# Weights converted in place, tokens mixed by rows, one rotated tile fewer and a new order of the start

## The chip, the cores and the metric

One Trainium2 chip; the program runs on one core. The metric is the device time of that core in microseconds, the median of several runs. TensorE (PE) does the matrix products, VectorE (DVE) and ScalarE (ACT) the elementwise work, GpSimd (POOL) a few small operations and the indirect loads, and SyncE (SP) issues the DMAs.

## The reference

Three layers follow each other on tensors of 4 batches, 768 tokens and 384 columns (8 heads of 48):

```python
# 1. attention with a complex decay, per batch and head
mag = np.sqrt(a_re * a_re + a_im * a_im)
scale = np.minimum(mag, 0.999) / (mag + 1e-06)
for t in range(S):                       # a = (a_re, a_im) * scale
    S_re, S_im = ar * S_re - ai * S_im + k_t v_t^T, ar * S_im + ai * S_re
    y[t] = q_t @ S_re
# 2. token mixing of rank 32, then an MLP 384 -> 1536 -> 384
u = x + (x.transpose(0, 2, 1) @ U @ V).transpose(0, 2, 1)
x = u + np.maximum(u @ w_ch1, 0.0) @ w_ch2
# 3. real part of a 2-D Fourier transform, normalisation, a second MLP
u = x + np.real(np.fft.fft(np.fft.fft(x, axis=1), axis=2))
un = (u - mean) / np.sqrt(var + 1e-06)
out = u + np.maximum(un @ w2_ch1, 0.0) @ w2_ch2
```

All inputs are float64 in memory (two 32-bit words a value) where they are weights, U and V, and float32 for the attention.

## The kernel before

**Pieces of work.** A batch has six chunks c of 128 tokens, and two groups g of three chunks (384 tokens). The attention works on pairs of chunks, numbered m: ACT and DVE make decays, phases, gains and from them a rotated tile QK (128 x 6 x 258; partition = position in a head's 16 columns and head, so 16 x 8). Six DMAs (`move`, L316) bring a QK to a tile QT (96 partitions, 8 heads x 258), each of them one of six blocks (z, i) to 16 neighbouring partitions. From QT come the scores (`sc`, L322), masked on DVE (`pm`), the outputs `y` (L337) and the states. The keys are turned back on PE (`kp`, L330), copied by head on ACT into a key tile (`kc`, L334; L371) and multiplied with the values (`g`). The rotated tiles have three buffers; the key tiles share a ring of three (`st`) with the loaded weights.

**Token mixing.** Six products on PE give z = U^T x of a batch (L384; U stands four times side by side, in parts), ACT copies it to `zst`, DVE subtracts for the low part. For a group and each of three column blocks k, PE transposes three chunks of x (`tokens`, L402), adds V^T z by one product (`mixed`, L414), and ACT and DVE split the result into two float16 tiles u (L1050, L1052): the mixed tokens, turned, are the moving operand of the first product. The residual x does not hold the mixing yet; so after the last second product three products `extra1` (L447) add it to the accumulator, for which ACT scales `zst` (`zsc`).

**MLP.** For each group and each of twelve blocks f (FB) of hidden columns: nine products in float16 parts (`first_product`, L192), ReLU on ACT (`hh`), its low part on DVE (`hl`), then six products with hh and three with hl into three accumulators (`second_product`, L208; L1083, L224). That is 18 matmuls of 384 columns for (group, f), 8 groups and 12 blocks, in both MLPs.

**Weights.** A float64 weight is made a float32 with integer steps (`word_steps`, L131): the sign and exponent word goes through Abs on ACT, the low word is shifted on DVE, and two DVE steps join them into a tile of its own (`slot`, ring `x1`); then ACT and DVE split it into two float16 parts (L163, L164). All this goes by tiles of 128 x 384, two for each (mi, f), 48 in all.

**Order.** The first six groups (batches 0 to 2 of the first MLP) with the attention of all batches are written in an order that is made when the program is built: `planned_start` (L616) describes each operation as a stream entry `op(engine, took, label, *after)`, and `planned` (L521) picks, engine by engine, the entry with the earliest known start plus a bias of its stream (`PLACES`, L486). Each engine and SP then run that order as it is; rings of buffers (`sizes`, L1184) count as waits. Where PE would idle over a unit, `warm_up` (L606) puts filler products in (L609 before the first MLP product, L612 after it). From group (3, 0) on, `moe_units` (L216) runs the rest: a side list (`put`, L1551) puts steps of the Fourier transform, of the last mixing (`make_ut(3, 1)`) and of the normalised inputs (`make_un`) at numbered half steps. `make_un` splits a normalised chunk into float16 parts and turns it with a DMA transpose (L1461).

Of the kernel before, what the change touches and what calls it, by code (L numbers as in the profile page):

```python
# [34 lines left out]
W1_MOST = 1.5  # L35
FOLD, WAVE = 2.0**6, 2.0**-3
# [12 lines left out]
def mixer_kernel(ctx, tc, a_in, qk_in, v_in, u_in, v4_in, w_in, cc_in, ss_in, cb_in, sb_in, id_in, mask_in, rows_in, out):  # L49
# [25 lines left out]

    def pair(name):
        if parts16[0]:
            return moe.tile([128, 2, 384], F16, tag="u", name=name, bufs=5)
        return pfl[0].tile([128, 2, 384], F32R, tag="u32", name=name, bufs=3)
# [45 lines left out]
    def fetch(src, name):  # L125
        n = src.shape[-1]
        st = moe.tile([128, 400, 2], I32, tag="st", name=f"st{name}", bufs=3)[:, :n]
        nc.sync.dma_start(st.rearrange("p n w -> p (n w)"), src.bitcast(I32))
        return st

    def word_steps(st, x):  # L131

        n = x.shape[-1]
# [13 lines left out]
    def words(mi, f, z):  # L147
        return w_in[mi, f][:, z * 384 : (z + 1) * 384], f"w{mi}_{f}_{z}"

    def load_steps(mi, f, z, st):  # L150

        if z == 0 and not parts16[0]:
            wt[mi, f] = wpl.tile([128, 2, 768], F32R, tag="w", name=f"w{mi}_{f}")
        elif z == 0:
# [3 lines left out]
        zs = slice(z * 384, (z + 1) * 384)  # L158
        hi, lo = wt[mi, f][:, 0, zs], wt[mi, f][:, 1, zs]
        x = slot(f"wx{words(mi, f, z)[1]}")  # L160
        if parts16[0]:
            return word_steps(st, x) + [
                ("A", lambda: A.activation(hi, x, AF.Copy, scale=WP[z])),  # L163
                ("V", lambda: V.scalar_tensor_tensor(out=lo, in0=x, scalar=WP[z], in1=hi, op0=ALU.mult, op1=ALU.subtract)),  # L164
            ]
        return word_steps(st, x) + [
            ("A", lambda: A.copy(hi, x)),
            ("G", lambda: G.tensor_tensor(lo, x, f32(hi), ALU.subtract)),
        ]

    def load_w(mi, f, z, st=None):
        for _, fn in load_steps(mi, f, z, fetch(*words(mi, f, z)) if st is None else st):
            fn()
# [8 lines left out]
    def weights(mi):  # L182
        todo = [(f, z) for f in range(FB) for z in range(2)]
        st = None
        for at, (f, z) in enumerate(todo):
            now = fetch(*words(mi, f, z)) if st is None else st
            st = fetch(*words(mi, *todo[at + 1])) if at + 1 < len(todo) else None
            load_w(mi, f, z, now)
            yield

# [25 lines left out]
    def moe_units(todo):  # L216
# [5 lines left out]
        def low(mi, b, g, f, hl, t):  # L222
            last_step = f == FB - 1
            T.matmul(acc[t], hl[:, TSS[t]], wt[mi, f][:, 0, 384:], start=False, stop=last_step and mi == 1)  # L224
            if last_step:
                if mi == 0:
# [75 lines left out]
    def qk_tile(kind, b, c):  # L302
        where = dict(pl=early[0], bufs=1) if c % 3 == 2 else dict(bufs=2)
# [30 lines left out]
    def by_head(ks, ps, z):  # L334
        A.copy(ks[:, :768].rearrange("t (h z x) -> t h z x", h=8, z=2)[:, :, z, :], ps.rearrange("t (x h) -> t h x", h=8))
# [1445 lines left out]
```

## Time and profile before

| | |
|---|---|
| median of 3 runs | 852.25 us (852.24 to 853.67) |
| profiled execution | 851.42 us, of it the span 849.6 us |
| PE busy | 789.3 us (93%), 6875 matmuls |
| DVE busy | 627.7 us (74%), 1304 instructions |
| ACT busy | 451.5 us (53%), 845 instructions |
| POOL busy | 36.7 us (4%) |
| DMA | 87.78 MB, mean 103 GB/s |
| granted TensorE clock | 0.996 of full speed |

The span runs from the first to the last instruction of the profile; the 1.8 us between it and the execution's time lie outside the program's instructions. Busy times are unions of an engine's instructions. A matmul's duration is the time until its result is there, and the next one starts long before that; on a full PE the distance of two starts is what one costs. Releasers (after an arrow) name what ended an engine's idle time.

### The profile page before, as it was taken

How to read it: one execution, taken by the hardware profiler on the slowest of the kernel's cores; microseconds unless marked ns; L12 is line 12 of the kernel's file. 1: busy time of each engine (PE TensorE's matmuls, PEld its weight loads, DVE VectorE, ACT ScalarE, POOL GpSimd, SP SyncE). 2: the span in 40 equal slices, each digit the busy share in tenths (PEclk: the TensorE clock that was granted, in tenths of full speed). 3: DMA queues.
4: the chain of work that ended last, by engine and by line, in shares of the span. 5: the costliest groups of instructions: out<-in, count | busy, mean ns of one | idle time of the engine just before them, and what ended most of it. 6: DMA issues, size and time to landing. Idle time of an engine off the chain costs nothing.

```text
span 849.6 us, 17219 instructions
## 1 busy us (share of the span) xinstructions
PE 789.3 (93%) x6875; PEld 533.1 (63%) x6875; DVE 627.7 (74%) x1304; ACT 451.5 (53%) x845; POOL 36.7 (4%) x79
## 2 busy tenths in 40 slices
PE   0298999999999999999999999999999999999996
PEld 0187755567766677666766666566666666666664
DVE  6989689998788986998965956666475748555653
ACT  7976597798868778848743252242215214321210
POOL 1001000000000010000002200001000100000000
PEclk9999999999999999999999999999999999999999
DMA  9539933487493494268675201211311142010100
GB/s 347 81 73 127 299 104 106 127 164 188 85 188 113 124 210 125 85 158 133 140 140 176 96 21 55 66 29 57 75 47 29 56 103 26 31 29 29 29 29 33
DMA packets 66553, 87.78 MB, mean 103 GB/s; under 512 B 24800, under 2 KB 55776, under 8 KB 66464
## 3 DMA queue, kind: packets, MB, share of 16 engines
q1 hardware_dynamic: 65184, 82.66, 41.0%
q0 software_dynamic: 1280, 3.93, 1.5%
q8 instruction: 56, 0.92, 0.5%
q14 instruction: 33, 0.27, 0.1%
HBM read 53.39 MB, written 9.44 MB: 74 GB/s over the span
## 4 chain that ended last, share of the span: by engine, by line
PE 77%; ACT 10%; DVE 6%; DMA 4%; issue 1%; SPq 1%; DVEq 0%; ACTq 0%
PE acc L210 10%; PE hp L105 10%; PE hp L107 10%; PE acc L211 10%; PE hp L106 10%; PE acc L224 7%; PE sc L325 4%; PE acc L1083 3%; PE y L343 3%; DMA QT<-QK 2%; ACT ain L101 2%; ACT L97 2%; PE g L343 2%; PE kp L332 1%; PE z L385 1%
## 5 line engine op out<-in xcount | busy, mean ns | idle before, releaser
L201 ACT ACTIVATE hh<-hp 128x384 f16<-128x384 f32 x192 | 93.3, 488 | 281.2 <-PE hp L107 270.1
L204 DVE SCALAR_TENSOR_TENSOR hl<-hp,hh 128x384 f16<-128x384 f32 x192 | 105.7, 555 | 126.4 <-ACT hh L201 125.7
L210 PE MATMUL acc<-w,hh 128*128 128x384 f16 x576 | 187.8, 327 | 3.5 <-ACT hh L201 3.4
L211 PE MATMUL acc<-w,hh 128*128 128x384 f16 x576 | 187.4, 326 | 0.0
L105 PE MATMUL hp<-u,w 128*128 128x384 f16 x288 | 94.3, 328 | 0.1
L106 PE MATMUL hp<-u,w 128*128 128x384 f16 x288 | 94.2, 327 | 0.0
L107 PE MATMUL hp<-u,w 128*128 128x384 f16 x288 | 94.2, 327 | 0.0
L105 PE MATMUL hp<-nt,w 128*128 128x384 f16 x288 | 94.1, 327 | 0.0
L107 PE MATMUL hp<-nt,w 128*128 128x384 f16 x288 | 94.0, 327 | 0.0
L106 PE MATMUL hp<-nt,w 128*128 128x384 f16 x288 | 94.0, 326 | 0.0
L210 PEld LDWEIGHTS <-hh 128*128 128x128 f16 x576 | 56.2, 98 | 41.5 <-ACT hh L201 6.1
L105 PEld LDWEIGHTS <-w 128*128 128x128 f16 x576 | 56.4, 98 | 37.8 <-issue 0.5
L107 PEld LDWEIGHTS <-w 128*128 128x128 f16 x576 | 56.3, 98 | 37.4 <-issue 0.2
L106 PEld LDWEIGHTS <-w 128*128 128x128 f16 x576 | 56.4, 98 | 36.8 <-issue 0.7
L211 PEld LDWEIGHTS <-hh 128*128 128x128 f16 x576 | 56.3, 98 | 34.1 <-issue 0.4
L224 PE MATMUL acc<-w,hl 128*128 128x384 f16 x360 | 77.6, 327 | 0.0
L325 PE MATMUL sc<-QT 96*128 96x128 f32 x384 | 50.1, 285 | 10.4 <-DMA QT<-QK 9.6
L325 PEld LDWEIGHTS sc<-QT 96*128 96x128 f32 x384 | 47.1, 198 | 12.8 <-issue 11.5
L332 PE MATMUL kp<-ident,QK 128*128 128x128 f32 x120 | 20.0, 294 | 33.4 <-DVE QK L309 31.1
L1083 PE MATMUL acc<-w,hl 128*128 128x384 f16 x216 | 49.2, 331 | 1.4 <-DVE hl L204 1.4
L224 PEld LDWEIGHTS <-hl 128*128 128x128 f16 x360 | 35.2, 98 | 23.7
L97 ACT ACT_TABLE_LOAD x33 | 42.3, 1283 | 1.3 <-PEq L1767 0.7
(262 smaller groups left out, 1395.3 us busy)
## 6 DMA issues: line engine op xcount, KB each, us to landing
QT<-QK SPq DMA_DIRECT2D x144, 129.0 KB, 6.8
stw<-in_w_dram SPq DMA_DIRECT2D x48, 384.0 KB, 5.2
ain<-in_a_dram SPq DMA_DIRECT2D x12, 768.0 KB, 6.9
qkin<-in_qk_dram SPq DMA_DIRECT2D x12, 768.0 KB, 6.3
x1d<-x SPq DMA_DIRECT2D x24, 192.0 KB, 4.1
vin<-in_v_dram SPq DMA_DIRECT2D x18, 192.0 KB, 3.9
lo<-x1d SPq DMA_DIRECT2D x12, 192.0 KB, 3.6
out_dram<-lo SPq DMA_DIRECT2D x12, 192.0 KB, 2.0
```

The lines of the kernel that those rows point to most:

```text
L97: ordered(lambda: A.preload_act_table_set(name))
L105: T.matmul(o, ah, bh, start=start, stop=False, skip_group_check=skip)
L106: T.matmul(o, ah, bl, start=False, stop=False, skip_group_check=skip)
L107: T.matmul(o, al, bh, start=False, stop=stop, skip_group_check=skip)
L201: A.activation(hh, hp, AF.Relu)
L204: V.scalar_tensor_tensor(out=hl, in0=hp, scalar=0.0, in1=whole_of(hh), op0=ALU.max, op1=ALU.subtract)
L210: T.matmul(acc[t], hh[:, TSS[t]], w[:, 0, 384:], start=f == 0, stop=False)
L211: T.matmul(acc[t], hh[:, TSS[t]], w[:, 1, 384:], start=False, stop=False)
L224: T.matmul(acc[t], hl[:, TSS[t]], wt[mi, f][:, 0, 384:], start=False, stop=last_step and mi == 1)
L325: T.matmul(ps[:, h, :], q[:, 128:256], q[:, :128], start=True, stop=True)
L343: T.matmul(out[p, hsl], l(h)[:, p], r[:, hsl], start=h == 0 and o + done == 0, stop=h == 7 and o + rest == len(ops) - 1, skip_group_check= ...
L1083: T.matmul(accs[t], hls[n][:, TSS[t]], wt[0, every[n][2]][:, 0, 384:], start=False, stop=False)
```

## The change

- Weights: a pair of tiles (768 columns) is loaded into one tile `dw` of a ring of two, by two DMAs, and made float32 in place: the shift, the sign and the last step on DVE write the low words, Abs on ACT the high words, each once over 768 columns. The split into float16 parts stays by 384. V is converted the same way in one piece, U in the buffer of `zst`. The slots of ring `x1` are not used for it any more.
- Rotated tiles: two buffers in place of three, so a chunk waits for the moves and the key turns of the chunk but one before it (instead of but two). QT keeps three.
- A move writes to every sixth partition of QT, starting at z * 3 + i, in place of 16 neighbouring ones; the columns of the key tile are laid out to match. The key tile has a buffer of its own, one, 768 columns wide, without the zeroed rest; so a chunk's key turns come after the state product of the chunk before.
- Mixing: U stands three times instead of four, z has 96 rows. Groups (0, 0), (0, 1) and (1, 0) are mixed as before. For (1, 1), (2, 0), (2, 1), (3, 0) and (3, 1) a product per chunk of tokens gives V^T z by rows, DVE adds it to x, ACT and DVE split the sum, and a DMA transpose turns it. For (1, 0) the product and the addition are made too, after the turned tiles have been read. `extra1` stays for batch 0 alone, as does the scaling of `zst`, which has one buffer now in place of two: its copy for batch 1 waits for the last `extra1` of batch 0, later ones for the last products by rows.
- `make_un(0, 0)`, the first normalised group, is turned by nine transposes on PE instead of three DMA transposes, at other half steps; `make_ut(3, 1)` is at half steps 11, 13 and 15.
- All biases of `PLACES` are others (two lines are shown), and the planner's costs for moves (1.0 to 0.62), for a DMA's start (2.4 to 2.15) and for early filler; so the order of the first six groups is another on every engine.

```diff
+    def turned_tile(name):
+        return moe.tile([128, 2, 3, 384], F16, tag="u", name=name, bufs=2)
...
+    def double_words(name):
+        return (attp[0] if parts16[0] else pfl[0]).tile([128, 768, 2], I32, tag="dw", name=f"st{name}", bufs=2 if parts16[0] else 1)
...
         low, high = st[:, :, 0], st[:, :, 1]
-        xi = x.bitcast(I32)
+        size = high.bitcast(F32)
         return [
-            ("A", lambda: kept(A.activation, x, high.bitcast(F32), AF.Abs, scale=2.0**-112)),
             ("V", lambda: kept(V.tensor_scalar, low, low, 29, None, ALU.logical_shift_right)),
-            ("V", lambda: V.scalar_tensor_tensor(out=xi, in0=xi, scalar=3, in1=low, op0=ALU.logical_shift_left, op1=ALU.bitwise_or)),
-            ("V", lambda: V.scalar_tensor_tensor(out=xi, in0=high, scalar=-(2**31), in1=xi, op0=ALU.bitwise_and, op1=ALU.bitwise_or)),
+            ("V", lambda: V.scalar_tensor_tensor(out=low, in0=high, scalar=-(2**31), in1=low, op0=ALU.bitwise_and, op1=ALU.bitwise_or)),
+            ("A", lambda: kept(A.activation, size, size, AF.Abs, scale=2.0**-112)),
+            ("V", lambda: V.scalar_tensor_tensor(out=low, in0=high, scalar=3, in1=low, op0=ALU.logical_shift_left, op1=ALU.bitwise_or)),
         ]
...
     def qk_tile(kind, b, c):
-        where = dict(pl=early[0], bufs=1) if c % 3 == 2 else dict(bufs=2)
+        where = dict(pl=early[0], bufs=1) if c % 3 == 2 and kind == "QT" else dict(bufs=2)
...
     def move(QT, QK, z, i):
-        p0 = z * 48 + i * 16
-        nc.sync.dma_start(QT[p0 : p0 + 16], QK[:, z, i, :])
+        nc.sync.dma_start(QT[z * 3 + i : 96 : 6], QK[:, z, i, :])
...
     def key_tile(n):
-        ks = moe.tile([128, 800], F32, tag="st", name=f"k{n}", bufs=3)
-        G.memset(ks[:, 768:], 0.0)
+        ks = attp[0].tile([128, 768], F32, tag="ks", name=f"k{n}", bufs=1)
...
+        for n in range(3):
             if parts16[0]:
-                A.activation(u[:, 0], xp, AF.Copy, scale=UP)
-                V.scalar_tensor_tensor(out=u[:, 1], in0=xp, scalar=UP, in1=u[:, 0], op0=ALU.mult, op1=ALU.subtract)
+                up = bank(f"up{b}_{g}_{n}")[:, :DM]
+                low_rank_back(up, b, 3 * g + n)
+                V.tensor_tensor(xt[b, 3 * g + n], up, xt[b, 3 * g + n], ALU.add)
+                n16 = split_tile(f"un{b}_{g}_{n}")
+                high_part(n16, xt[b, 3 * g + n])
+                low_part(n16, xt[b, 3 * g + n])
+                turn_over(nt, n16, n)
...
+    def low_rank_back(acc, b, c, start=True):
+        T.matmul(acc, vst[:96, c * 128 : (c + 1) * 128], zst[b][:96], start=start, stop=True)
...
+    def high_part(n16, x, scale=UP):
+        A.activation(n16[:, 0], x, AF.Copy, scale=scale)
+
+    def low_part(n16, x, scale=UP):
+        V.scalar_tensor_tensor(out=n16[:, 1], in0=x, scalar=scale, in1=n16[:, 0], op0=ALU.mult, op1=ALU.subtract)
+
+    def turn_over(nt, n16, t):
+        to = nt.rearrange("d z k t -> d (z k) t")[:, :, TSS[t]]
+        nc.sync.dma_start_transpose(out=to, in_=n16.rearrange("t z d -> t (z d)"))
...
-        "moves": (154, 157, 56),
+        "moves": (97, 209, 151),
...
+        "mixed_tokens": (-155, -109, -84),
...
-                free["Q"] = max(free["Q"], t + 2.4) + took
+                free["Q"] = max(free["Q"], t + 2.15) + took
...
-            for _ in range(int(us / 0.11)):
+            for _ in range(int(us / (0.11 if "sc2.0" in known else 0.15))):
...
-                if c > 2:
-                    before += [f"qt{c - 3}"] + ([f"kp{c - 3}.1"] if turned_too(c - 3) else [])
+                if c > 1:
+                    before += [f"qt{c - 2}"] + ([f"kp{c - 2}.1"] if turned_too(c - 2) else [])
...
-                    yield op("S", 1.0, f"qt{c}" if at_end else f"qt{c}.{z}{i}", *before)
+                    yield op("S", 0.62, f"qt{c}" if at_end else f"qt{c}.{z}{i}", *before)
...
-                yield op("P", 0.35, f"kp{c}.{z}", f"QKk{c}", "ident", *room_for(c), holds=[(ring, f"kc{c}.{z}")])
+                yield op("P", 0.35, f"kp{c}.{z}", f"QKk{c}", "ident", *room_for(c), *[f"g{x}" for x in (c - 1, c - 2)[: 1 + (c % NC == 0)] if x >= 0 and turned_too(x)], holds=[(ring, f"kc{c}.{z}")])
...
-            yield op("A", 0.42, f"zh{b}", f"z{b * NC + NC - 1}", *([f"ex{b - 2}.1.2"] if b > 1 else []))
-            z = zst[b] = xpl[0].tile([128, DM], F32R, tag="zst", name=f"zst{b}", bufs=2)
-            A.copy(z, zp)
+            yield op("A", 0.42, f"zh{b}", f"z{b * NC + NC - 1}", *([] if b == 0 else ["ex0.1.2"] if b == 1 else [f"up{b - 1}.1.{t}" for t in range(3)]))
+            z = zst[b] = xpl[0].tile([128, DM], F32R, tag="zst", name=f"zst{b}", bufs=1)
+            A.copy(z[:96], zp)
...
+        def mixed_tokens(b, g, t):
+            c = 3 * g + t
+            before = [f"hp1.0.{3 + 2 * t}"] if (b, g) == (1, 0) else [f"hp{b if g else b - 1}.{1 - g}.{(3, 5, 7)[t]}"]
+            yield op("P", 0.33, f"up{b}.{g}.{t}", f"zl{b}", *before, holds=[("ms", f"us{b}.{g}.{t}")])
+            up = bank(f"up_{b}_{g}_{t}")[:, :DM]
+            low_rank_back(up, b, c)
+            yield op("V", 0.5, f"us{b}.{g}.{t}", f"up{b}.{g}.{t}")
+            V.tensor_tensor(xt[b, c], up, xt[b, c], ALU.add)
+            if (b, g) == (1, 0):
+                return
...
+            high_part(n16, xt[b, c])
+            yield op("V", 0.5, f"ul{b}.{g}.{t}", f"uh{b}.{g}.{t}")
+            low_part(n16, xt[b, c])
+            yield op("S", TURN, f"ut{b}.{g}.{t}", f"ul{b}.{g}.{t}")
+            turn_over(nt, n16, t)
...
-                        yield op("P", 0.46, f"ex{b}.{g}.{t}", f"hl{name_of(n)}", f"zsc{b}")
+                        yield op("P", 0.17 if b else 0.46, f"ex{b}.{g}.{t}", f"hl{name_of(n)}", *([] if b else ["zsc0"]))
                         low(n, [t])
-                        extra1(b, g, t, accs[t])
+                        if b == 0:
+                            extra1(b, g, t, accs[t])
...
+            for n, (mi, f) in enumerate(pairs):
+                after = "v issued" if n < 2 else "qt3" if n < 4 else "qt5 issued" if n < FB else "hp{}.{}.{}".format(*pace(2 * n))
+                for z in range(2):
+                    yield op("S", 1.3, f"wl{n}.{z}", after, holds=[] if z else [("st", f"w{mi}.{f}.1")])
...
+                for k, took in enumerate((0.57, 0.87, 0.78, 0.87)):
+                    yield op("A" if k == 2 else "V", took, f"wc{n}.{k}", *([f"wc{n}.{k - 1}"] if k else [f"wl{n}.0", f"wl{n}.1"] + ([f"wc{n - 1}.3"] if n else [])))
+                    word_steps(loaded[n])[k][1]()
...
-        sizes = {"ms": 3, "acc": 3, "hid": 2, "st": 3, "x1": 3, "u": 5, "x": 10, "vin": 2}
+        sizes = {"ms": 3, "acc": 3, "hid": 2, "st": 2, "ks": 1, "x1": 3, "u": 2, "x": 10, "vin": 2}
...
-        if parts16[0]:
+        if parts16[0] and (b, g) != (0, 0):
             nt = ft(f"nt.{b}_{g}", [128, 2, 3, 384], F16, tag=("raw_cc", "raw_ss")[g])
...
+        first = turned_tile("n") if parts16[0] else None
...
-            u = pair(f"n{b}_{g}_{k}")
+            u = first[:, :, k] if parts16[0] else pair(f"n{b}_{g}_{k}")
...
-                put(make_ut(b, 1), (19, 21, 23))
-                put(make_un(0, 0), (41, 41, 42, 42, 43, 43))
+                put(make_ut(b, 1), (11, 13, 15))
+                put(make_un(0, 0), (41, 42, 42, 44, 45, 47))
```

## Rows read from the trace of the kernel before

**Rows 1.** The page's busy time of each engine, share of the span, instructions.

```profile
PE 789.3 (93%) x6875; PEld 533.1 (63%) x6875; DVE 627.7 (74%) x1304; ACT 451.5 (53%) x845; POOL 36.7 (4%) x79
```

**Rows 2.** Four stretches: busy us per engine (instructions), clock, DMA share, GB/s.

```profile
0.00:107.00 107.00, 64.65 (x871) 55.72 (x872) 87.75 (x150) 78.03 (x135) 6.43 (x25) 1.00 0.77 187
107.00:240.00 133.00, 124.72 (x1290) 86.87 (x1287) 117.98 (x193) 114.45 (x196) 2.92 (x12) 1.00 0.54 131
240.00:462.00 222.00, 219.62 (x2178) 153.07 (x2174) 180.09 (x304) 151.52 (x274) 10.73 (x22) 0.99 0.62 138
462.00:850.00 388.00, 380.28 (x2548) 237.45 (x2546) 241.85 (x659) 107.45 (x244) 16.58 (x20) 1.00 0.19 51
```

**Rows 3.** Instructions grouped by shape: xcount | busy us, mean ns | idle before.

```profile
L140 DVE SCALAR_TENSOR_TENSOR wxw<-stw,wxw 128x384 int32<-128x384 int32 x48 | 26.6, 555 | 0.7
...
L123 ACT ACTIVATE wxw<-stw 128x384 f32<-128x384 f32 x48 | 26.3, 551 | 10.4 <-DMA stw<-in_w_dram 10.3
...
L163 ACT ACTIVATE w<-wxw 128x384 f16<-128x384 f32 x48 | 24.6, 518 | 10.3 <-DVE wxw L140 10.1
...
L123 DVE TENSOR_SCALAR stw<-stw 128x384 int32<-128x384 int32 x48 | 16.9, 356 | 2.2 <-DMA stw<-in_w_dram 2.2
...
L775 ACT ACTIVATE ain<-ain 128x768 f32<-128x768 f32 x11 | 9.3, 842 | 8.5 <-DVE ain L877 8.5
...
L831 DVE SCALAR_TENSOR_TENSOR ain<-ls,ain 128x768 f32<-128x768 f32 x9 | 8.6, 955 | 2.5 <-ACT ain L757 2.4
...
L612 PE MATMUL acc<-ident,mask 128*128 128x128 f16 x127 | 8.2, 220 | 0.0
```

**Rows 4.** The chain of waits, 78 to 108 us: start, us, what.

```profile
77.62 0.97 DVE QK L309
...
86.30 9.31 DMA QT<-QK
...
103.49 0.45 ACT zst L1028
```

**Rows 5.** PE's instructions in time at three moments: start, us, what, [idle before].

```profile
75.72 2.02 PE L325 MATMUL sc<-QT 96*128 96x128 f32 x16 [1.35 <-DMA QT<-QK]
...
107.19 0.33 PE L105 MATMUL hp<-u,w 128*128 128x384 f16 x1
...
237.48 0.33 PE L105 MATMUL hp<-u,w 128*128 128x384 f16 x1
```

**Rows 6.** SP's queue in time, moves of chunks 4 and 5.

```profile
78.61 3.79 SPq L318 DMA_DIRECT2D QT<-QK  x6
...
83.62 4.06 SPq L318 DMA_DIRECT2D QT<-QK  x6
```

**Rows 7.** The tile QT, its moves from issue to landing.

```profile
DMA to landing us min/median/max: 3.0/6.8/10.0
```

**Rows 8.** Two stretches as in rows 2: moves alone, and loads.

```profile
31.00:40.40 9.40, 1.69 (x7) 0.89 (x5) 8.92 (x18) 9.12 (x15) 0.00 (x0) 1.00 0.91 113
...
100.00:107.00 7.00, 6.77 (x75) 5.43 (x76) 5.71 (x13) 6.84 (x18) 0.00 (x0) 1.00 1.03 410
```

**Rows 9.** PE in time on a saturated stretch, two kinds of small products.

```profile
460.58 0.82 PE L404 MATMUL xp<-ident,x 128*128 128x128 f32 x6
461.16 0.60 PE L415 MATMUL xp<-vst,zst 128*128 128x384 f32 x2
461.59 0.49 PE L404 MATMUL xp<-ident,x 128*128 128x128 f32 x3
```

**Rows 10.** Line L1461, DMA transposes: ns min/median/max, then issue to landing.

```profile
L1461 SPq DMA_TRANSPOSE nt<-n x24: 1211/1212/2003, 533.3 to 795.5; - x24
...
DMA to landing us min/median/max: 2.7/2.8/4.4
```

**Rows 11.** ACT in time, the copy of z of batch 1.

```profile
230.54 0.46 ACT L1028 CAST zst<-z 128x384 fp32r<-128x384 f32 x1
```

**Rows 12.** Waits of SP's queue, 107 to 462 us: total us, times, longest.

```profile
SPq L318 <- DVE QK L309: 40.7, 6, 15.3
```

More of the change, by code (lines that the diff above doesn't have):

```diff
@@ L35 @@
 W1_MOST = 1.5
+TURN = 0.66
 FOLD, WAVE = 2.0**6, 2.0**-3
@@ L157, in load_steps, with high_step, low_step @@
             wt[mi, f] = wboth[f][:, mi]
[L158 to L173, printed above, removed]
+        steps = []
+        for z in range(2):
+            zs = slice(z * 384, (z + 1) * 384)
+            hi, lo, x = wt[mi, f][:, 0, zs], wt[mi, f][:, 1, zs], word_values(st)[:, zs]
+            if parts16[0]:
+                def high_step(hi=hi, x=x, z=z):
+                    A.activation(hi, x, AF.Copy, scale=WP[z])
+                def low_step(hi=hi, lo=lo, x=x, z=z):
+                    V.scalar_tensor_tensor(out=lo, in0=x, scalar=WP[z], in1=hi, op0=ALU.mult, op1=ALU.subtract)
+                steps += [high_step, low_step]
+            else:
+                A.copy(hi, x)
+                G.tensor_tensor(lo, x, f32(hi), ALU.subtract)
+        return steps
     def check_w(mi, f, z):
@@ L182, in weights @@
     def weights(mi):
[L183 to L188, printed above, removed]
+        for f in range(FB):
+            st = double_words(f"{mi}_{f}")
+            fetch(w_in[mi, f], st)
+            for _, fn in word_steps(st):
+                fn()
+            load_steps(mi, f, st)
             yield
@@ new lines, in mixer_kernel @@
+        "more_tests": (0, -29, 81, 134, -169, 54, 55, 176, -150),
+        "moves": (97, 209, 151),
+        "score_steps": (126, -17, -175),
+        "mask_steps": (118, 43, -43),
+        "outputs": (55, -102, -166),
+        "key_turns": (-6, -138, -16),
+        "key_copies": (15, 23, 7),
+        "ends_of": (43, -2, -31),
+        "state_steps": (74, 6, -6),
+        "loads": (-66,),
+        "rank_words": (203, -41),
+        "mixing": (-3,),
+        "pieces": (-63,),
+        "mixed_tokens": (-155, -109, -84),
@@ L520, in mixer_kernel @@
+        "seconds": (-155,),
+        "firsts": (-122,),
+        "positives": (10,),
+        "positive_lows": (-6,),
+        "finishes": (-79,),
+        "word_loads": (-233,),
+        "word_conversions": (-13, 35),
+        "v_test": (96,),
+        "later_loads": (-55, 20),
+        "later_v": (27,),
     }
@@ L1082, in low @@
                 for t in ts:
-                    T.matmul(accs[t], hls[n][:, TSS[t]], wt[0, every[n][2]][:, 0, 384:], start=False, stop=False)
+                    f = every[n][2]
+                    T.matmul(accs[t], hls[n][:, TSS[t]], wt[0, f][:, 0, 384:], start=False, stop=f == FB - 1 and every[n][0] > 0)
             for n, (b, g, f) in enumerate(every):
@@ L1125, in accs_of @@
             return accs
-        tiles = [(mi, f, z) for mi in range(2) for f in range(FB) for z in range(2)]
+        pairs = [(mi, f) for mi in range(2) for f in range(FB)]
         loaded, left, begun = {}, [], [0]
@@ L1176, in planned_start @@
             streams.append((place("mixing"), mixing(b)))
-            streams += [(place("pieces"), pieces(b, g, k)) for g in range(2) for k in range(3) if (b, g) < (LATE, 1)]
+            streams += [(place("mixed_tokens", min(2 * b + g - 2, 2)), mixed_tokens(b, g, t)) for g in range(2) for t in range(3) if 0 < b and (b, g) < (LATE, 1)]
+        streams += [(place("pieces"), pieces(b, g, k)) for b, g in ((0, 0), (0, 1), (1, 0)) for k in range(3)]
         streams += [(place(x.__name__), x()) for x in (seconds, firsts, positives, positive_lows)]
```

230 lines of the change are left out of this document (104 added, 126 removed).

## Prediction

> **What bounds the kernel now.** I read the busy table first: TensorE (PE) is busy 789.3 us of 849.6 [rows 1], so its 60 idle us are the first question. The view by stretches places them: 42.3 lie before 107 us, 8.3 between 107 and 240, 2.4 between 240 and 462, and 7.7 after, most of them past the last product [rows 2]. So the kernel has three regimes. From 240 us on PE is the bound: what leaves PE there leaves the time. From 107 to 240 VectorE (DVE) is busy 118.0 and ScalarE (ACT) 114.5 of 133 us, and PE's busy time contains 8.2 us of filler, 127 matmuls of L612 [rows 3]. The first MLP of batch 1 cannot start before the attention of batch 1 has delivered its last chunk, so all three engines matter there. Before 107 us the end is set by the chain of waits.
>
> That chain ends so: the rotation of the sixth chunk of batch 0 on DVE (77.62), moves of the rotated tiles to QT from 78.61 on, the last landing at 86.30 + 9.31 = 95.61, then scores, output, z, its copy at 103.49 [rows 4], and the first MLP product at 107.19 [rows 5]. The 17.0 us from the first issue to that landing are the longest piece. SP issues the twelve moves of chunks 4 and 5 by 83.62 + 4.06 = 87.68 us [rows 6], though a move can land in 3.0 us [rows 7]: so the last one waits behind others in the DMA engines. In 31 to 40.4 us, when almost only moves run, the engines are busy 0.91 of the time and carry 113 GB/s; with loads spread over 128 partitions they carry 410 at 1.03 [rows 8]. A move's writes cost more than three times as much per byte.
>
> **Tokens mixed by rows, five groups.** Before, each (b,g) costs PE nine transposes, three `mixed` products and three `extra1` products. In the saturated stretch at 460.58 six transposes take until 461.16 (0.58, 0.097 each) and two `mixed` until 461.59 (0.43, 0.215 each) [rows 9]. For (1,1), (2,0), (2,1), (3,0) and (3,1) the nine transposes and three `mixed` go: 0.87 + 0.65 = 1.5 us a group. The three `extra1` become three `low_rank_back` with the same operands: nothing. (1,0) keeps its pieces, and exchanges the three products the same way. So 5 x 1.5 = 7.6 us leave PE, all after 240 us, where there is nothing to hide it: -7.6. `make_un(0,0)` moves from DMA to PE: nine transposes, +0.9. Its last piece is issued with one second product (nine matmuls) and six matmuls of the first product still ahead of its reader; that covers one ACT copy and one DVE subtraction of about 0.55 each. Sum on PE: -6.7.
>
> [...]
>
> What pays for it: 18 additions on DVE of about 0.55 (like the row of L140 [rows 3]), 9.9 us, 15 of them between 231 and 462, where DVE idles 42 of 222 us [rows 2]; 15 DMA transposes on SP, 1.21 us of queue each, landing 2.8 later where the trace has them [rows 10]. If DVE's cover were gone, the additions less what the conversions give back there (12 x 0.49) would cost 4.
>
> **Weights in place, 768 columns.** Before, a pair of tiles costs DVE 2 x (0.356 + 3 x 0.555) = 4.04 us (L139, L140 and L164 alike) and ACT 2 x (0.551 + 0.518) = 2.14 [rows 3]. After: one shift of 768 columns (0.36 to 0.71; I take the middle, 0.53), two steps at 0.955, two low parts at 0.555: 3.55; ACT 0.842 + 2 x 0.518 = 1.88. Saved: 0.49 and 0.26 a pair. Writing every other word costs nothing extra by the one row that does so: the shift, in place on 384 columns, takes 0.356. The upper bound, if it doubled a step, is +1.4 a pair. With V converted the same way DVE gives back 13 x 0.49 = 6.4 us and ACT 3.4 before 240 us; what is saved later (mi = 1) hides behind PE and counts nothing.
>
> **Moves to every sixth partition, and the head of the program.** No row shows a strided destination. Bounds for one move in a queue: as now, (17.0 - 3.0) / 11 = 1.27 us, or no more than SP's issue, (87.68 - 78.61) / 12 = 0.76 with the weight loads in between. The bytes now go to rows spread over 96 partitions, and the nearest row is the loads spread over 128 [rows 8], whose rate would need 0.3 us; so I take SP as the limit. Then the last move lands 9.1 + 3.0 = 12.1 us after 78.61 instead of 17.0: -4.9 at most at 107.
>
> [...]
>
> Whether 4.9 us survive until 240 depends on DVE and ACT, which must do the same conversions in less time. They get 6.4 and 3.4 us back. Between ACT's 3.4 and the chain's 4.9 I take **-4.0**; bounds 0 (all eaten by 240) and -8 (DVE's relief on top).
>
> **Waits that are added.** The rotated tile has two buffers, so chunk c waits for the moves and key transposes of c-2. Chunk 5 is the tight one: it rotates after 77.62, when chunk 3 has landed (its scores start at 75.72 [rows 5]); behind it stands all that DVE has in its order. Slack 2, price 0, at worst 3. One key tile: kp(c) now follows g(c-1) on PE, so a key turn and its copy on ACT come a state product later, and the state is needed only a chunk on: 0, at worst 1 us for each of the five of batch 0. One zst: its copy for batch 1 waits for the last `extra1` of batch 0. Behind it queue on ACT the splits of u, and PE waits for them: from the copy to the first product it is 107.19 - 103.49 = 3.7 us [rows 4, 5]. At this place the kernel already loses more: the copy comes at 230.54 [rows 11] and the product at 237.48 [rows 5], because z is late. So 0 now, but these 3.7 us stay if attention gets earlier. The POOL memsets that go were off the path. The new order itself: bounds by the PE slack of 107 to 240, 8.3 + 8.2 = 16.5 either way; value 0, since nothing in the trace shows it.
>
> **Sum.** -6.7 - 4.0 = -10.7 us. The profiled execution took 851.42 us (span 849.6 and 1.8 around it), 0.83 below the median of 852.25. 851.42 - 10.7 = 840.7, and at the level of the median 841.5. I predict **841.5**, its own range 837 to 846.
>
> **Rivals.** (1) The head gives nothing: strided moves land as now, or DVE and ACT eat it until 240. For it: ACT and DVE are at 86 and 89% there. Against: the relief above. -6.7: 845.6. (2) The order fills the gaps of 107 to 240: idle and filler 16.5, less the chain of 3.7 that the one zst keeps, less the 4.0 already counted, 8.8 more: 832.7. For it: DVE's relief; against: the z chain. (3) The other side: SP is one queue in order, and twelve transposes of the planned part stand in it behind moves that wait for DVE. The waits of moves for the rotation sum to 40.7 us in six, the longest 15.3 [rows 12]. A group's last tile may start after the eighth first product of the group before, four before its use: at the pace after 462 (388 us for 120 products, 3.2 each [rows 2]) that is 12.9 us; its own way (product 0.2, two DVE steps and one ACT step 1.6, SP 1.2, landing 2.8) takes 5.8, so slack is 7.1, and a wait of 15.3 in front costs 8.2 at the group's first product. One such group still leaves a gain; from two on (16.4, over the 10.7) it is slower: 857.9. Against: at the mean pace of 107 to 462 (355 us for 72, 4.9 each) the slack is 13.9. (4) Small stalls of the new order eat the gain: 852.
>
> **How the numbers follow.** Forecast 0.42, (1) 0.20, (2) 0.17, (3) 0.13, (4) 0.08. A measurement of this kernel tells 0.2%, 1.7 us, from no change. Faster 0.79, same 0.08, slower 0.13. The range from 829 to 852 leaves out (3) and a tail below (2).
>
> **What would show it.** Right: `xp` transposes down from 72 to 27 with nine new ones before 540 us; PE busy share still full after 240 and the time from the first product of (1,0) to the end shorter by about 6 to 7; moves landing with a median near 3 to 4 us instead of 6.8; first MLP product near 102; 3.5 us of DVE a weight pair. Wrong: QT landing as before (1); PE idle at the first product of (1,1), (2,0), (2,1) or (3,0) with the transposed tile as releaser (3); PE stalls of over 2 us at several other places (4); L612 and idle nearly gone before 240 (2).

## The result and the profile after

The changed kernel takes **864.05 us** (median of 4, 862.12 to 864.56) where the kernel before takes 852.25 (849.05 to 853.67): ratio 1.0131 [1.0101, 1.0161]. It is slower by 12 us; 10.7 us of gain were forecast. The profiled execution took 864.15, its span 862.4, so the spans differ by 12.8.

The page's busy times of the changed kernel, to be held against [rows 1]:

```profile
PE 793.3 (92%) x6852; PEld 534.7 (62%) x6852; DVE 629.8 (73%) x1246; ACT 458.7 (53%) x815; POOL 35.0 (4%) x59
```

PE is busy 4.0 us longer with 23 matmuls fewer, and ACT 7.2 longer with 30 instructions fewer. The four stretches of [rows 2] (bounds, length, busy us and instructions of PE, PEld, DVE, ACT, POOL, granted clock, DMA share, GB/s), for the changed kernel:

```profile
0.00:107.00 107.00, 67.90 (x848) 57.14 (x848) 89.60 (x133) 83.31 (x132) 5.33 (x20) 0.97 0.58 196
107.00:240.00 133.00, 123.36 (x1234) 86.17 (x1232) 109.90 (x162) 113.22 (x181) 1.66 (x5) 0.99 0.41 117
240.00:462.00 222.00, 215.31 (x2191) 150.50 (x2191) 183.13 (x283) 152.18 (x255) 6.97 (x10) 1.00 0.52 142
462.00:850.00 388.00, 381.03 (x2550) 237.64 (x2549) 244.60 (x667) 109.48 (x248) 21.05 (x24) 1.00 0.21 55
```

From 240 to 462, where PE idled 2.4 us, it now idles 6.7. The first products of the groups (start in us on PE's timeline; the last column is the first product of the second MLP) say where the 12.8 us go, and the best and the telling experiments stand beside them:

| kernel | (0,0) | (0,1) | (1,0) | (1,1) | (2,0) | (2,1) | (3,0) | (3,1) | 2nd MLP |
|---|---|---|---|---|---|---|---|---|---|
| before | 107.2 | 151.0 | 237.5 | 284.2 | 351.1 | 393.9 | 463.1 | 502.9 | 540.6 |
| after | 109.2 | 150.7 | 240.8 | 292.1 | 357.6 | 407.7 | 473.0 | 515.6 | 553.7 |
| before_step3 | 101.6 | 145.4 | 232.2 | 279.0 | 342.3 | 385.2 | 454.1 | 493.9 | 531.6 |
| after_step3 | 108.4 | 150.0 | 237.6 | 288.4 | 352.3 | 402.3 | 467.9 | 511.3 | 549.4 |
| a3_no_turn | 113.9 | 156.1 | 244.9 | 294.8 | 359.1 | 407.2 | 470.5 | 510.7 | 548.8 |
| a3_two_queues | 109.2 | 151.2 | 239.2 | 292.8 | 361.1 | 419.1 | 490.8 | 535.8 | 573.9 |
| a3_half_less | 102.0 | 144.5 | 231.8 | 282.7 | 350.4 | 403.6 | 469.0 | 511.0 | 549.1 |

So +2.0 us come until the first product, +1.3 until (1,0), +6.6 until (3,0), +3.2 until the second MLP, -0.3 after it. The loss is where PE work was removed. In that stretch, from (1,0) to the second MLP, the windows of before and then of after are:

```profile
237.48:540.60 303.12, 300.10 (x2745) 204.19 (x2743) 236.50 (x444) 180.42 (x337) 18.17 (x31) 0.99 0.52 123
```

```profile
240.80:553.70 312.90, 299.56 (x2757) 202.67 (x2755) 241.66 (x427) 181.77 (x320) 18.55 (x23) 1.00 0.46 127
```

Counted by the distance of PE's starts, what was to go did go: 45 transposes (4.6 us), 15 `mixed` (3.8) and 15 `extra1` (4.7), against 18 products by rows (4.9) and nine transposes of `make_un` (1.0). That is -7.2, where -6.7 was forecast. Two things ate most of it on PE itself, by the same count. The deferred products (`acc<-w,hl`) stand further apart, 35.8 us in place of 33.2 (the last ones before an idle stretch count in full). And the state products `g` of ten chunks take 12.6 us in place of 10.3: without the zeroed rest of the key tile, the last head's second product has 32 columns in place of 64, and the starts around it lie 59 to 152 ns apart where the others alternate between some 7 and 52. One chunk's state products, before and after:

```profile
290.78 1.14 PE L343 MATMUL g<-vin,k 128*64 128x48 f32 x32
```

```profile
259.92 1.33 PE L345 MATMUL g<-vin,k 128*64 128x48 f32 x32
```

Over the whole program that is 20.6 us before and 25.5 now, 4.9 us more of PE. Idle grew from 3.0 to 13.3 us (the windows above), and the 299.56 busy us hold 3.7 us of new filler. What PE waited for there, in the changed kernel (us, times, longest):

```profile
PE hp L107 <- DMA u<-un: 4.8, 4, 2.8
PE acc L211 <- ACT hh L202: 2.6, 3, 1.9
PE g L345 <- ACT k L336: 1.8, 3, 0.8
PE hp L107 <- DVE hl L205: 1.7, 1, 1.7
PE ac L109 <- DVE eel L1389: 1.4, 1, 1.4
```

The first row is the transposed tile. With the filler and the idle time just ahead, PE loses 0.75 us before (1,1), 4.0 before (2,0), 2.4 before (2,1) and 2.95 before (3,0): 10.1 us at the four groups that are turned by DMA within the planned part.

Group (3,0) shows why. Before, ACT copied z of batch 3 at 459.32; after, at 459.76, nearly the same moment. Its first product came 3.8 us later before (463.1), 13.3 later now. ACT, DVE, SP and PE of the changed kernel between the two (start, us, what):

```profile
459.76 0.47 ACT L1048 CAST zst<-z 96x384 fp32r<-96x384 f32 x1 [2.93 <-PE z L386]
...
464.73 0.55 ACT L166 ACTIVATE w<-st 128x384 f16<-128x384 f32 x1 [1.72 <-DVE st L141]
...
466.22 1.34 ACT L458 ACTIVATE un<-x 128x384 f16<-128x384 f32 x3
```

```profile
461.88 1.49 DVE L1088 TENSOR_TENSOR x<-up,x 128x384 f32<-128x384 f32 x3 [1.06 <-PE up L452]
...
466.86 1.49 DVE L461 SCALAR_TENSOR_TENSOR un<-x,un 128x384 f16<-128x384 f32 x3
```

```profile
467.44 3.93 SPq L465 DMA_TRANSPOSE u<-un  x3
471.59 0.40 SPq L1254 DMA_DIRECT2D rows<-in_rows_dram  x1
```

```profile
469.09 1.14 PE L1130 MATMUL acc<-w,hl 128*128 128x384 f16 x6
473.02 0.32 PE L107 MATMUL hp<-u,w 128*128 128x384 f16 x1 [2.79 <-DMA u<-un]
```

The reader is to see a chain in which the three chunks go together: three additions (1.5 us), 2.8 us until ACT is through the conversions and ReLUs ahead in its order, three high parts, three low parts, three transposes (3.9) and the landing. PE ran out of deferred products at 470.2. Group (2,0) has the same chain (z copied at 346.43, first product 11.1 us later). At (1,1) and (2,1) z had come 58 and 61 us before the first product; there the chunks stand together because ACT makes their high parts late in its order (from 283.47 and 399.54), and no run shows why it had to. The row behind the transposes matters too: the first loads of the Fourier transform stand in SP's queue behind them. Before, this load went out 9.2 us ahead of the group's first product,

```profile
453.93 0.33 SPq L1200 DMA_DIRECT2D rows<-in_rows_dram  x1
```

now 1.4 ahead of it. The wait for `hl` (1.7) in the list above, which ends at 485.0, hangs on this: DVE stands idle for the rows that these loads fetch, with `hl` behind in its order.

```profile
483.23 0.56 DVE L1333 TENSOR_TENSOR ye<-x,x 128x384 f32<-128x384 f32 x1 [3.00 <-DMA x<-x1d,rows]
```

The wait for `eel` (1.4, until 507.1) does not: it is 1.4 in a3_no_turn and a3_last_group_pe too (experiment 4), where no transpose of (3,0) stands ahead of the loads. There the first load leaves 3.0 and 3.5 us ahead of the product, not 9.2, since SP waits for the last weight's split on DVE (`w`, L169); so the transposes explain only a part of the delay.

### The profile page after: what moved, and what is told of

The parts are those of the page before. It is cut to its first block, busy times and chain, and to the rows that moved or that the text cites. A ratio compares the mean times of both kernels' runs of the same rounds, so it can differ in the third digit from the quotient of the medians.

```text
span 862.4 us, 17041 instructions
## 1 busy us (share of the span) xinstructions
PE 793.3 (92%) x6852; PEld 534.7 (62%) x6852; DVE 629.8 (73%) x1246; ACT 458.7 (53%) x815; POOL 35.0 (4%) x59
## 4 chain that ended last, share of the span: by engine, by line
PE 69%; ACT 14%; DVE 9%; DMA 5%; issue 2%; SPq 0%; POOL 0%; POOLq 0%; DVEq 0%; ACTq 0%
PE acc L211 10%; PE acc L212 9%; PE hp L107 9%; PE hp L109 9%; PE hp L108 9%; PE acc L225 6%; PE y L345 3%; PE sc L325 3%; PE acc L1130 2%; DMA ain<-in_a_dram 2%; PE g L345 2%; ACT L99 2%; ACT ain L103 2%; ACT k L336 1%; DMA u<-un 1%
## 5 line engine op out<-in xcount | busy, mean ns | idle before, releaser
L107 PE MATMUL hp<-nt,w 128*128 128x384 f16 x252 | 82.2, 326 | 0.0
L108 PE MATMUL hp<-nt,w 128*128 128x384 f16 x252 | 82.2, 326 | 0.0
L109 PE MATMUL hp<-nt,w 128*128 128x384 f16 x252 | 82.2, 326 | 0.0
L225 PE MATMUL acc<-w,hl 128*128 128x384 f16 x360 | 76.8, 326 | 0.0
L325 PE MATMUL sc<-QT 96*128 96x128 f32 x384 | 52.8, 288 | 5.3 <-DMA QT<-QK 5.3
L1130 PE MATMUL acc<-w,hl 128*128 128x384 f16 x216 | 46.9, 327 | 0.4 <-DVE hl L205 0.4
```

Source lines behind the costliest of these rows:

```text
L107: T.matmul(o, ah, bh, start=start, stop=False, skip_group_check=skip)
L108: T.matmul(o, ah, bl, start=False, stop=False, skip_group_check=skip)
L109: T.matmul(o, al, bh, start=False, stop=stop, skip_group_check=skip)
L325: T.matmul(ps[:, h, :], q[:, 128:256], q[:, :128], start=True, stop=True)
L1130: T.matmul(accs[t], hls[n][:, TSS[t]], wt[0, f][:, 0, 384:], start=False, stop=f == FB - 1 and every[n][0] > 0)
```

## The experiments

Two bases are used: before_step3, the kernel before with other moves, and after_step3, the changed kernel with the same moves. Ratios are to the kernel before on the same chip.

**1. Moves alone.** The order of the kernel before, with moves to every sixth partition, or to every third within a half; the key tile's columns follow.

```diff
-        p0 = z * 48 + i * 16
-        nc.sync.dma_start(QT[p0 : p0 + 16], QK[:, z, i, :])
+        nc.sync.dma_start(QT[z * 3 + i : 96 : 6], QK[:, z, i, :])              # step 6
+        nc.sync.dma_start(QT[z * 48 + i : z * 48 + 48 : 3], QK[:, z, i, :])    # step 3
```

> The kernel before with one edit: moves to every sixth partition and the key tile's columns laid out to match; the order of every engine is that of before. Theory K (key copies): with this layout a key copy on ACT takes 0.88 us in place of 0.48, 40 of them, 16 us in all, half of it before 240 us where ACT is full; the moves land in about 3.5 us in place of 6.8; the time rises to 856 to 862. Theory M (the prediction's step on the moves): 847 to 848. Theory R (the mixing by rows is what costs): no change, 851 to 853.

> The kernel before with moves to every third partition of a half, so that the columns of a key copy stay in runs of 48 words. Theory K: key copies near 0.48 us again, moves landing in 3.5 to 4.5 us, time 846 to 852. Theory M: 847 to 848. Theory R: no change. A key copy of 0.8 us or more here would say that it is the reading from the three blocks, not the writing by sixes, that is slow.

Measured: 845.75, 0.9916 [0.9886, 0.9946], and **842.11, 0.9876 [0.9824, 0.9927]**: faster than both kernels. The moves of before land in a median of 6.8 us [rows 7], with step 6 in 3.5, with step 3 in 4.7. The key copies (instructions, busy us and mean ns, idle before) of before, of step 6 and of step 3:

```profile
L335 ACT COPY k<-kp 128x384 f32<-128x384 f32 x40 | 17.6, 476 | 10.5 <-PE kp L332 8.4 <-PE g L343 2.0
```

```profile
L335 ACT COPY k<-kp 128x384 f32<-128x384 f32 x40 | 32.1, 879 | 6.0 <-PE kp L331 5.9
```

```profile
L335 ACT COPY k<-kp 128x384 f32<-128x384 f32 x40 | 17.5, 476 | 6.4 <-PE kp L331 6.3
```

With step 6 the copy writes single words 24 bytes apart, with step 3 runs of 48 words. A copy of step 6 whose order makes runs of three words,

```diff
-        to = ks[:, :768].rearrange("t (h x z i) -> t z h i x", h=8, z=2, i=3)
-        A.copy(to[:, z], ps.rearrange("t (i x h) -> t h i x", i=3, h=8))
+        to = ks[:, :768].rearrange("t (h x z i) -> t z h x i", h=8, z=2, i=3)
+        A.copy(to[:, z], ps.rearrange("t (i x h) -> t h x i", i=3, h=8))
```

> The kernel of before_step6, where a key copy runs through its 384 words in the order head, x, i in place of head, i, x: it writes runs of three words in place of single words 24 bytes apart. If the distance of neighbouring writes is what costs, a copy takes 0.6 us or less in place of 0.88, and the time falls from 845.8 to 842 to 844. If each run has its price whatever its length, 0.6 to 0.7 and 843 to 845; if not, 0.88 and 845 to 847.

took 842.50, 0.9893 [0.9851, 0.9934], with 559 ns a copy. So the copies cost 3.3 to 3.6 us at the old order, and step 6 and step 3 are then alike.

**2. The changed kernel with these moves, and with the old ones.**

> The changed kernel with moves to every third partition and key copies in runs of 48 words; nothing else. Theory K: key copies near 0.48, ACT busy about 15 us less, time 852 to 857 (7 to 12 below the changed kernel). Theory R: within 2 us of the changed kernel, 862 to 865, with PE still waiting at the first products of (1,1), (2,0), (2,1) and (3,0) for the turned tile.

> The changed kernel with moves to 16 neighbouring partitions and key copies in runs, as before the change; nothing else. Theory K: copies 0.48, moves landing in 6 to 7 us, time 853 to 860, below the changed kernel all the same. Theory M: 867 to 869, above it by the 4 to 5 us that the moves are worth. Theory R: 862 to 866.

Measured: 861.33, 1.0111 [1.0054, 1.0169], and 888.65, 1.0417 [1.0358, 1.0475]. By the medians the copies cost 2.7 us at the new order, which is inside the spread of after_step3 (859.53 to 865.40). The new moves, at the new order, are worth 27.3 where 4 to 5 were expected, with a granted clock of 0.974 and 0.991 in the two profiles. Most of what makes the kernel slower is elsewhere.

**3. What PE work is worth.** before_step3 without its 24 `extra1`.

```diff
-                        extra1(b, g, t, accs[t])
```

> The kernel of before_step3, its order unchanged, with the 24 products extra1 left out (the residual of the first MLP lacks the mixing then). Theory P (the prediction's: after 240 us what leaves PE leaves the time): 18 of them after 240 us at 0.215 us are 3.9, so 842.1 falls to 837 to 839. Theory C (from 240 us on the attention, which DVE and ACT deliver, sets the time as much as PE): the time stays within 1.5 us, 840.5 to 843.

Measured: 840.40, 0.9854 [0.9799, 0.9908]: 1.7 us less. The stretch from (1,0) to the second MLP with its 15 products, before_step3 first, then without them:

```profile
232.20:531.60 299.40, 298.05 (x2745) 203.35 (x2743) 236.31 (x444) 180.28 (x337) 18.87 (x31) 1.00 0.46 125
```

```profile
231.50:529.80 298.30, 295.75 (x2730) 201.48 (x2729) 236.04 (x444) 180.45 (x337) 16.19 (x31) 1.00 0.46 125
```

By the distances 15 x 0.31 = 4.7 us went. PE's busy time falls by only 2.3, since the deferred products beside them stand further apart (32.7 us before, 34.5 without), and idle grows by 1.2: the stretch is 1.1 us shorter. The whole run's 1.7 is of the order of the spreads (841.21 to 844.50, and 840.20 to 841.34).

**4. The turn by DMA.** In after_step3 the transposes of the four groups are left out (a zeroed tile takes their place); a second kernel leaves out the filler L632 too.

```diff
             turned_of[b, g] = turned_tile(f"u_{b}_{g}")
+            if (b, g) > (1, 0):
+                G.memset(turned_of[b, g].bitcast(F32), 0.0)
...
             yield op("S", TURN, f"ut{b}.{g}.{t}", f"ul{b}.{g}.{t}")
-            turn_over(nt, n16, t)
```

> The kernel of after_step3, its order unchanged, with the DMA transposes of groups (1,1), (2,0), (2,1) and (3,0) left out: their turned tile is filled with zeros by GpSimd when it comes free, so the first products read no mixed tokens, and wait for none. Theory R (the chain by rows is what the four groups wait for): in after_step3 PE loses 1.0, 4.0, 2.4 and 3.0 us ahead of their first products, 3.7 of it filler that stays here, and 3 us to the late loads of the Fourier transform; so 861.3 falls to 851 to 855. Rival C (the attention sets the time, and the wait comes back elsewhere): 859 to 862.

> As a3_no_turn, and the filler products of L632 are left out too (164 in after_step3, 10.2 us, 3.7 of it after 240 us). Theory R: the filler stood where PE would have waited for the turned tile; with the wait gone it costs its own 3.7 us: 847 to 851. Rival C: no further change, or more if the granted clock falls.

Measured: 855.90, 1.0043 [1.0019, 1.0067], and 857.78, 1.0082 [1.0050, 1.0113]. The stretch from (1,0) to the second MLP, after_step3 first, then a3_no_turn:

```profile
237.60:549.40 311.80, 301.20 (x2757) 203.03 (x2755) 241.64 (x427) 175.96 (x320) 16.08 (x23) 0.99 0.49 127
```

```profile
244.90:548.80 303.90, 298.78 (x2757) 202.64 (x2755) 241.71 (x427) 175.75 (x320) 20.86 (x27) 1.00 0.46 123
```

It is 7.9 us shorter with the same PE instructions, and the median falls by 5.4 (the intervals of the two ratios just overlap). The profile of a3_no_turn is the slowest of its ten runs: its granted clock is 0.63 from 60 to 80 us, where nothing was edited, and the head ends 5.5 us later. In a3_no_turn_no_fill, whose head is as in after_step3 (first product at 108.2), the stretch takes 305.2 us, 6.6 less. In the medians, leaving out the filler too gains nothing. The reverse test makes the chain longer: the second transpose of a group goes to ACT's queue, which I had expected to shorten it.

```diff
-        nc.sync.dma_start_transpose(
+        (nc.sync, nc.scalar, nc.sync)[t].dma_start_transpose(
```

> The kernel of after_step3, where the second of the three DMA transposes of a group is issued by ACT's queue. Theory R (the chain by rows): the three stand in a row in SP's queue for 3.9 us; with one of them beside the others the turned tile comes 1.3 us earlier at four groups, PE's waits for it fall from 5.1 us to 2 or less, time 857 to 860. Rival: ACT, which issues it in its order, delays hh by as much: 860.5 to 863.

Measured: 879.17, 1.0298 [1.0248, 1.0347]. Each transpose starts 2.9 us after the one of the other queue, about the 2.8 that one takes to land [rows 10]. Its queues ahead of (1,1), and what PE waited for from 237 to 550:

```profile
283.98 7.05 SPq L465 DMA_TRANSPOSE u<-un  x2
286.91 1.34 ACTq L465 DMA_TRANSPOSE u<-un  x1
```

```profile
PE hp L107 <- DMA u<-un: 14.4, 4, 5.7
```

Some 3 us more from the first to the last transpose (7.05 against 3.9; 8.34 at (2,1)) raise the waits for the tile at the four groups from 5.1 us in after_step3 to 14.4: the chain is on the path at all of them. The 17.8 us of time are not this alone. From (1,0) to the second MLP the granted clock is 0.95, against 0.99, and PE is busy 11.5 us longer; and ACT, which issues one of the three in its order, stands idle for 2.8, 2.6 and 1.8 us behind the first three. Turning only (3,0) on PE again,

```diff
-            if (b, g) == (1, 0):
+            if (b, g) in ((1, 0), (3, 0)):   # pieces by nine transposes and three products on PE
                 return
```

> The kernel of after_step3, where only group (3,0) gets its turned tile from PE again (nine transposes and three products, 1.5 us of PE) and not from three DMA transposes, which stand in SP's queue ahead of the first loads of the Fourier transform. Theory Q (SP's queue): the loads leave about 15 us earlier, and PE's waits for the turned tile (2.8 us), for hl (1.1) and for eel (1.4) go: 855 to 859 in place of 861.3. Rival (the transposes are not what is late): 861 to 864, the 1.5 us of PE on top.

gave 861.79, 1.0115 [1.0076, 1.0153]: no change in the median of nine runs from 858.14 to 866.56. In its profile, the fastest of them, (3,0) to (3,1) falls from 43.4 to 40.3 us, and 1.9 us are left at the second MLP (547.5 against 549.4).

**5. Order, buffers, head.** after_step3 with the biases of before; before_step3, planned anew, with two rotated tiles.

```diff
-        "moves": (97, 209, 151),
+        "moves": (154, 157, 56),    # and all other biases of before
```

```diff
-        where = dict(pl=early[0], bufs=1) if c % 3 == 2 else dict(bufs=2)
+        where = dict(pl=early[0], bufs=1) if c % 3 == 2 and kind == "QT" else dict(bufs=2)
```

> The kernel of after_step3 with the biases of the kernel before wherever both have them; the operations, buffers and costs are those of after_step3. Theory O (the order decides): the time moves by 20 us or more, with the same busy times of DVE and ACT. Rival (the order is worth little, as the prediction took it): 858 to 865.

> The kernel of before_step3 with two rotated tiles in place of three; biases and costs unchanged, the planner makes its order anew. Theory B (the buffers cost): 848 or more, with the first products of (1,0) and (1,1) late. Rival (price 0, as predicted): 841 to 844.

Measured: 904.39, 1.0600 [1.0519, 1.0681], and 863.59, 1.0122 [1.0049, 1.0194]. The new order is 43 us better than the old biases for the changed operations. Two rotated tiles with the order that follows cost 21.5 us, of them only 0.8 until (1,0) (233.0) and 25 by (1,1) (304.2). Buffer and order are not separated by this.

The head: half of the early filler between the scores of chunk 2 and the first product; 12 conversions without their sign step; dense filler (0.11) in the changed kernel; thin filler (0.15) in before_step3.

```diff
-            for _ in range(int(us / (0.11 if "sc2.0" in known else 0.15))):
+            for _ in range(int(us / (0.22 if "sc2.0" in known else 0.15))):   # a3_half_fill, a3_half_less
+            for _ in range(int(us / 0.11)):                                   # a3_fill11
...
-                    word_steps(loaded[n])[k][1]()
+                    if mi or k != 1:                                          # a3_less_conversion, a3_half_less
+                        word_steps(loaded[n])[k][1]()
```

> The kernel of after_step3, its order unchanged, where the conversion of the first MLP's twelve weight pairs leaves out the step that joins the sign (0.96 us of DVE each, so these weights lose their sign). Theory D (until 240 us DVE sets the pace, and the conversions stand ahead of the masks of chunks 3 to 5): the first product of the MLP comes 3 to 6 us earlier than 108.4, that of (1,0) 5 us or more earlier than 237.6. Rival: the conversions run beside other work, and both move by less than 1.5 us.

> The kernel of after_step3 with the early filler as dense as in the kernel before (0.11 us of planned idle time for one product in place of 0.15), order unchanged. Theory F (the thinner filler lets TensorE's clock fall): the granted clock in 60 to 80 us goes from 0.91 back to 1.00, the first product of the MLP comes 1 to 3 us earlier than 108.4, time 858 to 860.5. Rival (the order alone): 108 to 109, and 860.5 to 862.5.

> The kernel of before_step3 with the thinner early filler of the changed kernel, order unchanged. Theory F: a granted clock below 1.00 somewhere before 107 us, the first product 1 us or more after 101.6, time 843 to 846. Rival: 841 to 843.

> The kernel of after_step3 with half the filler between the scores of chunk 2 and the first MLP product (0.22 us of planned idle time for one product), order unchanged. Theory M (in the head PE waits for masks that DVE does behind conversions, and the filler in between hides what DVE gains): the first product at 107 to 108.5, time 860 to 862. Rival (the filler itself is in the way): 106 or earlier. If the granted clock falls below 0.9 in 80 to 120 us, 110 or later, and 863 or more.

> As a3_half_fill, and the conversions of the first MLP's weights leave out the step that joins the sign, as in a3_less_conversion. Theory M: the masks come 1 to 3 us earlier, and so does the first product, 105 to 106.5; what follows keeps 1 to 3 us. Rival (DVE is not what the head waits for): as a3_half_fill within 0.7 us.

| kernel | us | ratio | first product |
|---|---|---|---|
| a3_less_conversion | 861.67 | 1.0119 [1.0064, 1.0174] | 108.5 |
| a3_fill11 | 864.54 | 1.0127 [1.0079, 1.0175] | 107.2 |
| b3_fill15 | 842.11 | 0.9882 [0.9849, 0.9916] | 101.5 |
| a3_half_fill | 863.71 | 1.0131 [1.0106, 1.0156] | 111.5 |
| a3_half_less | 860.46 | 1.0101 [1.0041, 1.0160] | 102.0 |

Shorter conversions alone do not move the head (with a granted clock of 0.83 from 60 to 80 us, against 0.91 in after_step3), and denser filler hardly does (a3_fill11). Whether less filler alone does is not shown: a3_half_fill's profile has a granted clock of 0.60 from 60 to 80 us, so its head cannot be compared. Both together do: a3_half_less reaches the head of before_step3. The clock is not the reason, as it is 1.00 from 60 to 80 us in a3_fill11 too, whose first product comes at 107.2. But the 6.4 us of a3_half_less at the first product (5.8 at (1,0)) are gone at (2,1): 403.6 against 402.3, where PE waits for `hh` (3.0) and for an input load of the attention (1.9). A kernel with two queues, dense filler and (3,0) on PE at once (a3_combined) took 877.11, 1.0297 [1.0261, 1.0334], where 854 to 859 was expected, and tells no more than a3_two_queues.

## Why the prediction was wrong

The time came nearest to rival (3), 857.9, which had a chance of 0.13.

**PE's work.** The terms that the sum has were sized right (-7.2 for -6.7). The 36 transposes fewer are 3.6 us of it, 0.10 each by the distance of the starts. The step that failed is "From 240 us on PE is the bound: what leaves PE there leaves the time". In experiment 3, 4.7 us of products left out shortened the stretch by 1.1 and the time by 1.7. In the changed kernel the waits and the filler at four turned groups, 10.1 us, stand against the 7.2.

**The chain by rows** failed in its size. Rival (3) had the right place, PE idle at the first products of turned groups with the transposed tile as releaser, at one or two groups of 8.2 us each; it happened at four, of 0.75 to 4.0. It failed in its cause too: no wait of a move stood in front on SP. My "own way" of 5.8 us was that of one chunk alone, with its predecessors done. The chunks go together, and at (2,0) and (3,0) behind z: 13.3 us at (3,0) against 3.8 before. I had the z chain in hand ("because z is late") and did not put the new pieces behind it. "1.21 us of queue each" missed the Fourier loads behind the transposes, 1.7 us of waits.

**Moves**: the direction was right and the term too small. The forecast, -4.9 at most at 107 and -4.0 until 240, is -5.6 and -5.3 in before_step3 (-4.0 and -2.1 in before_step6, with its slow copies), and the time of before_step3 falls by 10.4, since the moves of later chunks gain too (-8.8 at (2,0)). The prediction saw only the head. In the changed kernel, the moves of the tile QT land as fast as forecast (median near 3 to 4):

```profile
DMA to landing us min/median/max: 2.3/3.4/9.9
```

That rows farther apart land sooner stands in the landing times (medians of 6.8, 4.7 and 3.5 us in experiment 1); why, no run shows.

**Missed altogether**: "the columns of the key tile are laid out to match". The copies went from 476 to 877 ns, 14.7 us more of ACT,

```profile
L336 ACT COPY k<-kp 128x384 f32<-128x384 f32 x40 | 32.3, 877 | 10.5 <-PE kp L332 10.3
```

and 2.7 us of the time by the medians (experiment 2). The words "without the zeroed rest" hid a second price, the 4.9 us of PE on the state products; the sum has no term for it, and no run takes it out alone.

**Conversions** cost as forecast: grouped by shape (mean ns ahead of the second bar), 0.555 + 0.958 + 0.954 + 2 x 0.553 = 3.57 on DVE for 3.55, and 0.909 + 2 x 0.545 = 2.0 on ACT for 1.88.

```profile
L125 DVE TENSOR_SCALAR st<-st 128x768 int32<-128x768 int32 x24 | 13.3, 555 | 1.5 <-DMA st<-in_w_dram 1.5
...
L139 DVE SCALAR_TENSOR_TENSOR st<-st 128x768 int32<-128x768 int32 x24 | 23.0, 958 | 0.7
...
L125 ACT ACTIVATE st<-st 128x768 f32<-128x768 f32 x24 | 21.8, 909 | 14.8 <-DVE st L139 12.5 <-issue 2.2
```

A step of a conversion is now one block of 0.96 in an order in which short steps wait behind it; that this alone costs time is not shown, as a3_less_conversion leaves out one such step and keeps its head. In the head, PE of the changed kernel runs 33 filler products and starts the batch's last outputs after them, while the masks on DVE stand behind two conversions:

```profile
94.83 0.55 DVE L125 TENSOR_SCALAR st<-st 128x768 int32<-128x768 int32 x1
95.42 0.96 DVE L139 SCALAR_TENSOR_TENSOR st<-st 128x768 int32<-128x768 int32 x1
96.30 0.68 DVE L328 TENSOR_TENSOR room<-sc,mask 128x512 f32<-128x512 f32 x1
```

```profile
94.44 3.77 PE L629 MATMUL warm<-ident,mask 128*128 128x256 f16 x33
...
109.22 0.34 PE L107 MATMUL hp<-u,w 128*128 128x384 f16 x1
...
116.87 0.34 PE L211 MATMUL acc<-w,hh 128*128 128x384 f16 x1 [4.55 <-ACT hh L202]
```

**Open**: with fast copies the changed kernel is still 19.2 us above before_step3 (861.33 - 842.11), and the turn by DMA holds 5.4 of them (7.9 in its stretch). The rest, some 11 to 14, may lie in the order, the buffers, the state products (4.9 us of PE) and the granted clock (0.991 against 0.998 of the span); no run separates these. So whether the order's "value 0" was wrong stays open; experiment 5 shows only that two orders of the same operations can lie 43 us apart. An estimate for the clock: over the ten runs of a3_no_turn the time falls 0.60 us for each 0.001, so 0.007 would be 4 us; but the clock of the changed kernel also fell, to 0.50, after PE had idled for 4.55 us (the last point below), so it may in part be an effect.

## What to carry to other kernels

Before counting removed matmuls as time, follow the new operand's whole way from its late input to its first reader with all its parts in the same group, and ask what stands ahead on each engine and what stands behind on each queue. When a layout is changed to please one mover, price every other instruction that writes or reads it: here a copy went from 476 to 877 ns. A part that pays by itself (the moves, 10 us) is found by trying it alone at the old order.

## What the runs showed that was not expected

- Moves of sixteen rows to partitions six apart land in a median of 3.3 to 3.5 us, three apart 4.7, neighbours 6.6 to 6.8.
- An ACT copy of 128 x 384 words takes 476 ns in runs of 48 words, 559 in runs of three, 877 to 879 as single words 24 bytes apart. It is the writing that costs: single words are read in the order of the kernel before, whose copy takes 476, and runs of three in that of step 3, which takes 476 too. Writing every other word, as the conversions do, cost DVE nothing extra (954 to 958 ns against 955 in the row of L831) and ACT little (909 against 842 in that of L775) [rows 3]. Why the words 24 bytes apart cost so much more, no run shows.
- A narrower product cost more here: with the last head's second product of 32 columns in place of 64, a chunk's state products take 1.27 us of PE in place of 1.03 (by the starts, mean of 20 chunks).
- Transposes on two DMA queues went one after the other: 2.9 us from one start to the next (283.98, 286.91), where one queue issues three in 3.9.
- After the 4.55 us of idle PE that end at 116.87, ten products from 117.26 on start 0.32 us apart in place of 0.16, and the granted clock is 0.50 from 117.3 to 120.4 (0.93 from 100 to 120). From 120.7 on they are 0.16 apart again. In before_step3 the clock is 1.00 there.
